# Two attention layers in one kernel: two pairs of scores in four banks under one exponential, the third pair first and copied

## The chip, the cores and the metric

The kernel runs on one core of one Trainium2 chip. The metric is device time in microseconds (us) of one launch, the median of the runs of a kernel. The engines are called as the profile's page calls them: PE (TensorE, matmuls), PEld (its weight loads), ACT (ScalarE), DVE (VectorE), POOL (GpSimd), SP (SyncE, which issues most DMAs).

## The reference

Two attention layers over 2048 tokens of 576 columns, 32 heads of 18, all in float32. Layer A has one key and value head shared by all query heads and no mask. Layer B has keys and values for every head, runs over four segments of 512 tokens with a causal mask inside a segment, and mixes in a memory of earlier segments. The two results stand side by side.

```python
# layer A
scores = jnp.einsum("bhqd,bkd->bhqk", q, k) * (Dh ** -0.5)
p = _softmax(scores, axis=-1)
o = jnp.einsum("bhqk,bkd->bhqd", p, v)
return (lambda x, *d: x.transpose(*d))(o, 0, 2, 1, 3).reshape(B, S, H * Dh) @ wo
...
# layer B, for each segment s
logits = jnp.einsum("bhqd,bhkd->bhqk", qs, ks) * scale + mask
p = _softmax(logits, axis=-1)
a_dot = jnp.einsum("bhqk,bhkd->bhqd", p, vs)
...
o = g * a_mem + (1.0 - g) * a_dot
...
return jnp.concatenate([a, b], axis=-1)
```

## The kernel before

The kernel has three stages. The first (up to about 281 us) projects queries, keys and values of both layers and builds B's memory. The second, attention, is the one that the change is in. The third (from about 1356 us) multiplies the last chunks by the output weights.

**Blocks and pairs.** Attention goes block by block. A block is four heads by 512 queries (`("A", c, hg)` or `("B", s, hg)`); there are 32 of each layer, and B's are put between A's early ones by the list `after`. A block of A has 16 key tiles of 128 keys. The four heads are two *pairs*, and the scores of one pair for one key tile are 128 x 1024 numbers (two heads by 512 queries) in two PSUM banks. So a block of A has 32 pairs. A block of B has three key tiles and six pairs. The mask leaves the first tile's pairs with 2 x 512 columns and the others' with 2 x 384, the third holding two short tiles side by side.

**Turns.** The pairs of a block are cut into *turns* of three. Since 32 is no multiple of three, a block of A has ten turns of three and a last one of two; a block of B has two turns. That makes 320 + 32 + 64 = 416 turns. `manual_schedule` fixes the order on PE, ACT and DVE as the loop over `k` writes it. In turn `k`:

- `scores` writes, for each pair, the score matmuls into a tile E of two banks (L890 for A, L898 for B). The pool `psE` has three such tiles, six of the eight banks. The other two are O (products) and F (other matmuls, one bank).
- The turn's second pair (`copied`) is copied by DVE from E to the SBUF tile W (L905), so that E is free before ACT gets to it. ACT then makes the exponential from W (L908). The first and third pairs are read by ACT straight from E (L908). ACT's order in a turn is first, third, second.
- In some places of A (`BY_DVE`: two fixed ones in each block, and a third where nothing else is due) DVE makes the exponential of half a pair itself, with seven operations on 512 columns (L864 to L871). ACT then takes only the other 512 columns, from W to the tile PD.
- B's exponentials are masked on the diagonal by POOL (L913).
- One step of other work follows from `run_fill` (mostly F: the output projection of finished chunks, L741, 8 matmul records a turn).
- Then the products of probabilities and values for the items of turn `k - 2` (`products`, L938): three items of four matmuls, each matmul in two records, into O. At a block's end DVE copies O out (L947).
- `due` places other steps that have become due: loads, sums, and POOL's weighing of finished heads (L725). A weighing step is held back near turns of B and while DVE's operations of an exponential are outstanding (`slow`).

Because the score of a turn goes into three tiles that come free one by one, PE may write the first pair of the next turn while ACT is still at this one's later pairs. Probabilities go to nine tiles P and two tiles PD, and the order of key tiles in the products (`turn_of`) lets DVE's slow ones come later.

Of the kernel before, what the change touches and what calls it, by code (L numbers as in the profile page):

```python
# [8 lines left out]
F32 = mybir.dt.float32  # L9
F32R = mybir.dt.float32r  # L10
# [22 lines left out]
BOUND_OK = 30.0 / SCALE / BOUND_UP  # L33
PBUFS = 9
KP = 54
# [13 lines left out]

LOG2 = SCALE * 1.4426950408889634  # L50
EXP_A = LOG2 * 2.0 ** 23
EXP_B = (127.0 + math.log2(0.00011720523372930181)) * 2.0 ** 23
POLY = [1.0925606709321247, 32.334180715292455, 88.7610992882796, 4291.093056129828]
MANTISSA, ONE_BITS, EXPONENT = 0x7FFFFF, 0x3F800000, 0xFF800000

BY_DVE = {(0, 1): 5, (5, 0): 12, (9, 1): 15}
THIRD = (9, 1)
QALL = [(slice(0, 36, 2), 0), (slice(1, 36, 2), 1), (slice(36, 54), 0)]
# [19 lines left out]
def attention_pair_kernel(ctx, tc, a_xT, a_w, a_wo, b_xT, b_w, b_wo, b_beta, ident_d, hmask_d, bmask_d, cmask_d, sel_d, zmask_d, selx_d, sely_d, out):  # L78
# [552 lines left out]
    pa = at_.enter_context(tc.tile_pool(name="pa", bufs=1, reuse_waits="tile"))  # L631
    psE = at_.enter_context(tc.tile_pool(name="psE", bufs=3, space=PSUM, reuse_waits="tile"))
    psO = at_.enter_context(tc.tile_pool(name="psO", bufs=1, space=PSUM, reuse_waits="tile"))
    attention = at_

# [220 lines left out]

    slow, now, gate, third = [], [0], [], set()
    AFTER = mybir.DependencyInfo(mybir.DependencyClass.Sync, mybir.DependencyReason.SCHED_ONLY)

    def exponentials(p, e, whole):  # L860

        u, w = (pp.tile([128, 512], F32, name=nm, bufs=1) for nm in "nq")
        v, stt, y = nc.vector, nc.vector.scalar_tensor_tensor, p.bitcast(U32)
        v.tensor_scalar(y, e, EXP_A, EXP_B, op0=ALU.mult, op1=ALU.add)  # L864
        ops = [
            lambda: v.tensor_scalar(u.bitcast(U32), y, MANTISSA, ONE_BITS, op0=ALU.bitwise_and, op1=ALU.bitwise_or),
            lambda: v.tensor_scalar(w.bitcast(U32), y, EXPONENT, None, op0=ALU.bitwise_and),
            lambda: stt(p, u, POLY[0], u, op0=ALU.add, op1=ALU.mult),
            lambda: stt(p, p, POLY[1], u, op0=ALU.add, op1=ALU.mult),
            lambda: stt(p, p, POLY[2], p, op0=ALU.add, op1=ALU.mult),  # L870
            lambda: stt(p, p, POLY[3], w, op0=ALU.add, op1=ALU.mult),  # L871
        ]
        slow.extend((now[0] + 2 + i, p, ops[2 * i : 2 * i + 2], whole) for i in range(3))

    def scores(it, pr, copied):

        ab, c, hg, kt = it
        st = stacks[ab, c, hg // 2]
        h = 2 * (hg % 2) + pr
        e = psE.tile([128, 2, 512], F32, name="E")  # L880
        if ab == "A" and (kt, pr) == THIRD and not any(cost and k <= now[0] + 4 for k, cost, *_ in later):
            third.add((c, hg))
        dve = ab == "A" and (kt, pr) in by_dve(c, hg)
        p = pp.tile([128, 2, 512], F32, name="PD" if dve else "P", bufs=2 if dve else PBUFS)
        state[it, pr] = p
        n = 512 if ab == "A" else 512 - 128 * kt if kt < 2 else 384
        if ab == "A":
            for j, r0 in enumerate(HALF):
                rows = slice(r0, r0 + KR)
                nc.tensor.matmul(e[:, j], kstA[rows, 128 * kt : 128 * kt + 128], st[rows, h, :], start=True, stop=True)  # L890
            if dve:
                exponentials(p[:, 0], e[:, 0], p)
        else:
            for k, c0 in BKEYS[kt]:
                ks = slice(128 * k, 128 * k + 128)
                for j, r0 in enumerate(HALF):
                    rows = slice(r0, r0 + KR)
                    nc.tensor.matmul(  # L898
                        e[:, j, c0 : c0 + 512 - 128 * k], st[rows, 4 + h, ks], st[rows, h, 128 * k :], start=True, stop=True
                    )  # L900
        src, hs = e, slice(0, 2)
        if copied:
            src = pp.tile([128, 2, 512], F32, name="W", bufs=2)
            hs = slice(1, 2) if dve else slice(0, 2)
            gate.append(nc.vector.tensor_copy(src[:, hs, :n], e[:, hs, :n]))  # L905

        def exponential():
            nc.scalar.activation(p[:, hs, :n], src[:, hs, :n], AF.Exp, scale=SCALE)  # L908
            if ab == "B":

                m = len(BKEYS[kt])
                diag = p.rearrange("p a (b t) -> p a b t", t=256)[:, :, 0:m, 0:128]
                nc.gpsimd.affine_select(  # L913
                    diag, diag, pattern=[[0, 2], [0, m], [1, 128]], base=0, channel_multiplier=-1, compare_op=ALU.is_ge, fill=0.0
                )

        return exponential

    acc, ready = {}, []

    def products(b, m, hf):
# [7 lines left out]
        for j in range(4):  # L929
            kt = turn_of(c, hg)[j // 2][m] if ab == "A" else m  # L930
            p = state[b + (kt,), j // 2]
            assert all(x[3] is not p for x in slow)
# [5 lines left out]
            nc.tensor.matmul(  # L938
                o[32 * j : 32 * j + 32, q0 : q0 + n],
                v,  # L940
                p[:, j % 2, p0 : p0 + n],
                start=m == hf == 0,
                stop=last and hf == 1,
            )
# [10 lines left out]
        return None  # L955


    def by_dve(c, hg):

        return [x for n, x in enumerate(BY_DVE) if n < 2 or (c, hg) in third]  # L960

    def turn_of(c, hg):

        order = []
        for pr in range(2):
            ks = [kt for kt in range(NKT) if (kt, pr) not in by_dve(c, hg)]
            for kt, p_ in by_dve(c, hg):
                if p_ == pr:
                    ks.insert(BY_DVE[kt, p_], kt)
            order.append(ks)  # L970
        return order

# [24 lines left out]
    def due(k, most=2, heavy=2):  # L997

        cost = 0

        near = [its[n][0] for t in turns[k : k + 3] for n, pr in t]
        heavy *= "B" not in near and not slow
        for e in [e for e in later if e[0] <= k]:
            if most and cost + e[1] <= heavy and e[2]():
                later.remove(e)
                e[3](k)
                cost += e[1]
                most -= 1
        return cost
# [66 lines left out]
    with tc.manual_schedule(engines={ENG.PE, ENG.Activation, ENG.DVE}):  # L1076
# [36 lines left out]
        def repeat(key):  # L1113

            o = parts[key]
            raws[key] = pp.tile([128, 2, 512], F32, name="PD", bufs=2)[:88, 0]
# [26 lines left out]
        def halve_heads(key, t):  # L1143
            R = RT[t]
            x = halves_of[key, t] = pp.tile([128, 2, 512], F32R, name="P", bufs=PBUFS)
            if t < 4:
                halve(x[:R, 0], x[:R, 1], parts[key][:R, t])
                return
            hi = pp.tile([128, 2, 512], F32R, name="PD", bufs=2)
            mixed(x[:, 0], hi[:, 0], parts[key][:, 4], some[:, 0:1])  # L1150
            mixed(x[:88, 1], hi[:88, 1], raws[key], some[:88, 1:2])

        for k in range(len(turns) + 2):
            now[0] = k
            exps = [scores(its[n], pr, i == 1) for i, (n, pr) in enumerate(turns[k])] if k < len(turns) else []
            for i in (0, 2, 1) if len(exps) == 3 else range(len(exps)):
                exps[i]()
            if k in (2, 4, 6):
# [17 lines left out]

            ends = k > 1 and any(hf and its[n][3] == (NKT - 1 if its[n][0] == "A" else 2) for n, hf in prods[k - 2])
            if slow and (slow[0][0] <= k or not ends):
# [73 lines left out]
        def eight_banks():  # L1252
            banks = [psE.tile([128, 2, 512], F32, name="E") for _ in range(3)]
            dst = [bk[:, hf, :288] for bk in banks for hf in range(2)]
            return dst + [psO.tile([128, C], F32, name=nm)[:, :288] for nm in ("O", "F")]

        def evict(osb, hf, src):
            (nc.vector.tensor_copy if hf else nc.scalar.copy)(osb[:, hf], src)

        dst = eight_banks()  # L1260
        for t in range(5):
# [17 lines left out]
        for g in range(8):  # L1279
# [4 lines left out]
            if not hf:  # L1284
                osb = pp.tile([128, 2, 512], F32, name="P", bufs=PBUFS)[:, :, :288]
            evict(osb, hf, dst[g])
# [234 lines left out]
```

## Time and profile before

| | |
|---|---|
| median of 3 runs | 1398.92 us (1397.57 to 1401.16) |
| the profiled execution | 1397.32 us, of which the span is 1395.4 us |
| granted TensorE clock | 0.999 |
| turns in attention | 416 |
| exponential instructions at L908 | 1216 (800 from E, 416 from W) |
| DVE's copies to W at L905 | 416 |

In the rows, `P<-E` is an instruction that writes P and reads E, with the shapes behind it, `x` the count, and the releaser of an idle time stands behind an arrow. Durations of neighbours on an engine can overlap, so the distance between two starts tells what one takes in a stream.

### The profile page before, as it was taken

How to read it: one execution, taken by the hardware profiler on the slowest of the kernel's cores; microseconds unless marked ns; L12 is line 12 of the kernel's file. 1: busy time of each engine (PE TensorE's matmuls, PEld its weight loads, DVE VectorE, ACT ScalarE, POOL GpSimd, SP SyncE). 2: the span in 40 equal slices, each digit the busy share in tenths (PEclk: the TensorE clock that was granted, in tenths of full speed). 3: DMA queues.
4: the chain of work that ended last, by engine and by line, in shares of the span. 5: the costliest groups of instructions: out<-in, count | busy, mean ns of one | idle time of the engine just before them, and what ended most of it. 6: DMA issues, size and time to landing. Idle time of an engine off the chain costs nothing.

```text
span 1395.4 us, 41198 instructions
## 1 busy us (share of the span) xinstructions
PE 1382.5 (99%) x17455; PEld 835.6 (60%) x17455; DVE 1033.2 (74%) x1512; ACT 1204.4 (86%) x1494; POOL 261.1 (19%) x382
## 2 busy tenths in 40 slices
PE   9999999999999999999999999999999999999998
PEld 6787887755554555555555555555555555555558
DVE  6655454477787788787888877876879778887884
ACT  4543553499999999999999999999999999999992
POOL 2443221003312211412110122113010220001002
PEclk9999999999999999999999999999999999999999
DMA  9766656576465445332312452232103321120013
GB/s 288 259 216 196 191 178 206 175 210 189 146 182 172 139 149 158 101 113 78 112 59 71 141 160 56 91 115 83 52 34 94 111 76 39 32 73 21 18 63 133
DMA packets 89022, 173.67 MB, mean 124 GB/s; under 512 B 12308, under 2 KB 20621, under 8 KB 88402
## 3 DMA queue, kind: packets, MB, share of 16 engines
q1 hardware_dynamic: 81902, 159.22, 36.6%
q0 software_dynamic: 2176, 6.51, 1.6%
q10 hardware_dynamic: 4752, 5.23, 1.1%
q8 instruction: 139, 2.28, 0.7%
q14 instruction: 53, 0.43, 0.1%
HBM read 99.65 MB, written 70.67 MB: 122 GB/s over the span
## 4 chain that ended last, share of the span: by engine, by line
PE 88%; DVE 5%; ACT 4%; issue 2%; DMA 1%; SPq 0%; POOL 0%; DVEq 0%; ACTq 0%
PE O L938 32%; PE E L890 20%; PE F L741 11%; PE pj L259 11%; ACT P L908 4%; PE E L898 3%; PE nd L496 2%; PE pj L496 2%; DVE W L905 2%; PE E L1222 2%; PE pj L291 1%; PE F L797 1%; PE tr L422 0%; DVE sm L690 0%; DMA stB<-qB 0%
## 5 line engine op out<-in xcount | busy, mean ns | idle before, releaser
L908 ACT ACTIVATE P<-E 128x1024 f32<-128x1024 f32 (+1 forms) x800 | 788.1, 1076 | 1.6 <-PE E L890 1.3
L905 DVE COPY W<-E 128x1024 f32<-128x1024 f32 (+2 forms) x416 | 453.2, 1089 | 143.1 <-PE E L890 84.2
L938 PE MATMUL O<-P,VA 128*32 128x256 f32 x7504 | 507.1, 379 | 0.0
L908 ACT ACTIVATE P<-W 128x1024 f32<-128x1024 f32 (+1 forms) x330 | 369.9, 1121 | 6.3 <-DVE W L905 5.6
L938 PEld LDWEIGHTS O<-P,VA 128*32 128x32 f32 x7504 | 259.0, 110 | 137.7 <-issue 4.3
L890 PE MATMUL E<-xl,kstA 56*128 56x512 f32 x1920 | 317.2, 430 | 2.1 <-ACT P L908 1.9
L890 PEld LDWEIGHTS E<-xl,kstA 56*128 56x128 f32 x1920 | 155.0, 184 | 159.1 <-issue 94.8
L913 POOL TENSOR_SCALAR_AFFINE_SELECT P<-P 128x256 f32<-128x256 f32 (+1 forms) x192 | 95.0, 495 | 412.5 <-ACT P L908 403.3
L725 POOL TENSOR_TENSOR xh<-xh,rb 126x512 f32<-126x512 f32 (+1 forms) x55 | 72.9, 1350 | 425.9 <-DVE PD L871 185.1
L741 PE MATMUL F<-woB,xh 126*32 126x192 f32 (+1 forms) x1920 | 126.6, 338 | 0.0
L938 PE MATMUL O<-PD,VA 128*32 128x256 f32 x688 | 88.9, 379 | 0.0
L741 PEld LDWEIGHTS F<-woB,xh 126*32 126x32 f32 (+1 forms) x1920 | 38.6, 108 | 74.9 <-issue 69.9
L938 PE MATMUL O<-P,vseg 128*32 128x256 f32 (+2 forms) x1536 | 81.4, 344 | 0.1
L947 DVE COPY oe<-O 128x512 f32<-128x512 f32 x64 | 44.3, 692 | 42.3 <-PE O L938 40.4
L259 PE MATMUL pj<-xh,wBl 128*126 128x512 f32 x180 | 71.9, 400 | 0.4 <-issue 0.4
L864 DVE TENSOR_SCALAR PD<-E 128x512 uint32<-128x512 f32 x86 | 59.2, 688 | 17.6 <-PE E L890 15.8
L259 PE MATMUL pj<-xh,wBh 128*126 128x512 f32 x180 | 71.6, 398 | 0.5 <-DVE xh L219 0.5
L124 ACT CAST qp<-pj 126x512 fp32r<-126x512 f32 (+1 forms) x54 | 31.1, 585 | 46.9 <-DVE kmB L454 41.8
L741 PE MATMUL F<-woA,xh 126*32 126x192 f32 (+1 forms) x960 | 63.9, 338 | 0.0
L938 PEld LDWEIGHTS O<-P,vseg 128*32 128x32 f32 x1536 | 48.8, 109 | 24.4 <-issue 1.9
L898 PE MATMUL E<-stB 56*128 56x256 f32 (+3 forms) x512 | 61.5, 348 | 2.0 <-ACT P L908 1.5
L871 DVE SCALAR_TENSOR_TENSOR PD<-PD,q 128x512 f32<-128x512 f32 x86 | 59.5, 692 | 3.0
(228 smaller groups left out, 1544.0 us busy)
## 6 DMA issues: line engine op xcount, KB each, us to landing
stB<-kB SPq DMA_DIRECT2D x96, 144.0 KB
stB<-qB SPq DMA_DIRECT2D x32, 288.0 KB
xl<-qA SPq DMA_DIRECT2D x30, 288.0 KB
oA<-oe SPq DMA_DIRECT2D x32, 256.0 KB
oB<-oe SPq DMA_DIRECT2D x32, 256.0 KB
qA<-qp SPq DMA_DIRECT2D x16, 504.0 KB
kB<-qp SPq DMA_DIRECT2D x16, 504.0 KB
qB<-qp SPq DMA_DIRECT2D x16, 504.0 KB
```

The source lines that it names most:

```text
L259: nc.tensor.matmul(dst, w[:, c0 : c0 + M], x, start=i == 0, stop=i == len(ops) - 1)
L496: nc.tensor.matmul(pj[:, :n], x, w, start=m == 0, stop=m == len(ops) - 1)
L725: ins = tc.keep_in_program_order(nc.gpsimd.tensor_tensor(dst, a, b, op=op))
L741: nc.tensor.matmul(dst[32 * j : 32 * j + 32], parts[ab, c][: RT[t], t, r0 : r0 + 32], wo[ab][: RT[t], t, c0 : c0 + n], start=start, stop=stop,
L864: v.tensor_scalar(y, e, EXP_A, EXP_B, op0=ALU.mult, op1=ALU.add)
L871: lambda: stt(p, p, POLY[3], w, op0=ALU.add, op1=ALU.mult),
L890: nc.tensor.matmul(e[:, j], kstA[rows, 128 * kt : 128 * kt + 128], st[rows, h, :], start=True, stop=True)
L898: nc.tensor.matmul(e[:, j, c0 : c0 + 512 - 128 * k], st[rows, 4 + h, ks], st[rows, h, 128 * k :], start=True, stop=True)
L905: gate.append(nc.vector.tensor_copy(src[:, hs, :n], e[:, hs, :n]))
L908: nc.scalar.activation(p[:, hs, :n], src[:, hs, :n], AF.Exp, scale=SCALE)
L913: nc.gpsimd.affine_select(diag, diag, pattern=[[0, 2], [0, m], [1, 128]], base=0, channel_multiplier=-1, compare_op=ALU.is_ge, fill=0.0)
L938: nc.tensor.matmul(o[32 * j : 32 * j + 32, q0 : q0 + n], v, p[:, j % 2, p0 : p0 + n], start=m == hf == 0, stop=last and hf == 1,)
```

## The change

The three tiles of two banks become one tile E2 of two banks and one tile E4 of four. In a turn of three pairs, two pairs of one key tile share E4, and the remaining pair has E2. `scores` takes the whole turn:

- The single pair is the third of the turn if the turn begins with a pair 0, else the first. Its matmuls come first. DVE copies it from E2 to W.
- Then the four score matmuls (for B's third tile eight) of the two others go into E4, and ACT makes one exponential over all four banks (2048 columns; 1536 for B's narrower tiles), from E4 to a tile P4.
- ACT's order in a turn is the wide exponential, then the one from W. A turn of two pairs has the wide one alone.
- POOL masks the wide pair in one instruction.
- DVE makes no exponentials: `exponentials`, `by_dve`, `turn_of`, the tables for them and the list `slow` are gone, and the products run in plain order of key tiles.

P becomes four tiles P4 and four tiles P2. Around the end, tiles that used the names P, PD and E take the new ones, and the output products get a pool of their own (`psN`) once the score banks are given back. The core of the diff:

```diff
-    def scores(it, pr, copied):
-
-        ab, c, hg, kt = it
-        st = stacks[ab, c, hg // 2]
-        h = 2 * (hg % 2) + pr
-        e = psE.tile([128, 2, 512], F32, name="E")
...
-        p = pp.tile([128, 2, 512], F32, name="PD" if dve else "P", bufs=2 if dve else PBUFS)
...
+    def scores(items):
+
+        pairs = [its[n] + (pr,) for n, pr in items]
+        single = [] if len(items) < 3 else [2 if items[0][1] == 0 else 0]
+        double = [i for i in range(len(items)) if i not in single]
+        todo = []
+        for group in (single, double):
+            if not group:
+                continue
+            w = 2 * len(group)
+            e = psE.tile([128, w, 512], F32, name=f"E{w}")
+            p = pp.tile([128, w, 512], F32, name=f"P{w}", bufs=PXBUFS if w == 4 else PBUFS)
...
+            for g, i in enumerate(group):
+                ab, c, hg, kt, pr = pairs[i]
...
+                state[its[items[i][0]], pr] = p[:, 2 * g : 2 * g + 2]
...
+                        e[:, 2 * g + j], kstA[rows, 128 * kt : 128 * kt + 128], st[rows, h, :], start=True, stop=True
...
+            src = e
+            if w == 2:
+                src = pp.tile([128, 2, 512], F32, name="W", bufs=2)
+                gate.append(nc.vector.tensor_copy(src[:, :, :n], e[:, :, :n]))
+            todo.append((p, src, n, w, len(BKEYS[kt]) if ab == "B" else 0))
+        for p, src, n, w, m in todo[::-1]:
+            nc.scalar.activation(p[:, :, :n], src[:, :, :n], AF.Exp, scale=SCALE)
...
-    psE = at_.enter_context(tc.tile_pool(name="psE", bufs=3, space=PSUM, reuse_waits="tile"))
+    psE = scored.enter_context(tc.tile_pool(name="psE", bufs=1, space=PSUM, reuse_waits="tile"))
...
-        heavy *= "B" not in near and not slow
+        heavy *= "B" not in near
...
-            for op in slow.pop(0)[2]:
-                gate.append(op())
```

How the instructions stand on PE in one turn of a block of A (c = 2, hg = 3, its fourth turn), with the engines that each first one waits for. Before, the turn's three pairs each have an E of their own, F follows, and then the products O:

```order
L890 MATMUL E_13342<-xl_11530,kstA_119 128x512 [waits Activation_49]
L890 MATMUL E_13342<-xl_11530,kstA_119 128x512
L890 MATMUL E_13346<-xl_11530,kstA_119 128x512 [waits DVE_49]
L890 MATMUL E_13346<-xl_11530,kstA_119 128x512
L890 MATMUL E_13355<-xl_11530,kstA_119 128x512 [waits Activation_49]
L890 MATMUL E_13355<-xl_11530,kstA_119 128x512
L741 MATMUL F_13250<-woB_4643,xh_10641 32x192 x4
```

Now (the next turn of the same block, in which the last product group stands behind a wait; E4 and E2 are the score tiles, P4 and P2 the probabilities):

```order
L875 MATMUL E2_12013<-xl_10400,kstA_119 128x512 [waits DVE_49]
L875 MATMUL E2_12013<-xl_10400,kstA_119 128x512
L875 MATMUL E4_12019<-xl_10400,kstA_119 128x512 [waits Activation_49]
L875 MATMUL E4_12019<-xl_10400,kstA_119 128x512 x3
L734 MATMUL F_11996<-woB_4421,xh_9630 32x192 x4
L916 MATMUL O_11968<-P4_11955,VA_120 32x256 x8
L916 MATMUL O_11968<-P2_11949,VA_120 32x256 x2
L916 MATMUL O_11968<-P2_11982,VA_120 32x256 [waits Activation_49]
L916 MATMUL O_11968<-P2_11982,VA_120 32x256
```

The copied pair moved from second to first, and the other two stand behind one wait for ACT. The last products read P2_11982, which ACT writes in the turn just before, as its last exponential.

On ACT, the same places. Before, two turns:

```order
L908 ACTIVATE P_13343<-E_13342 128x1024 [waits PE_49]
L908 ACTIVATE P_13356<-E_13355 128x1024 [waits PE_49,Activation_49]
L908 ACTIVATE PD_13347<-W_13353 128x512 [waits DVE_49]
L908 ACTIVATE P_13381<-E_13380 128x1024 [waits PE_49,Activation_49]
L908 ACTIVATE P_13391<-E_13390 128x1024 [waits PE_49]
L908 ACTIVATE P_13385<-W_13388 128x1024 [waits DVE_49]
```

Now, three turns:

```order
L891 ACTIVATE P4_11988<-E4_11987 128x2048 [waits PE_49,Pool_49]
L891 ACTIVATE P2_11982<-W_11985 128x1024 [waits DVE_49,Pool_49]
L891 ACTIVATE P4_12020<-E4_12019 128x2048 [waits PE_49,Activation_49]
L891 ACTIVATE P2_12014<-W_12017 128x1024 [waits DVE_49]
L891 ACTIVATE P4_12050<-E4_12049 128x2048 [waits PE_49,Activation_49]
L891 ACTIVATE P2_12044<-W_12047 128x1024 [waits DVE_49]
```

Three exponentials of a turn became two, and none of 512 columns is left.

More of the change, by code (lines that the diff above doesn't have):

```diff
@@ L854, in load_vseg @@
         vseg[s] = v
-    slow, now, gate, third = [], [0], [], set()
+    now, gate = [0], []
     AFTER = mybir.DependencyInfo(mybir.DependencyClass.Sync, mybir.DependencyReason.SCHED_ONLY)
[L860 to L873, printed above, removed]
@@ L875, in scores @@
-    def scores(it, pr, copied):
-        ab, c, hg, kt = it
-        st = stacks[ab, c, hg // 2]
-        h = 2 * (hg % 2) + pr
-        e = psE.tile([128, 2, 512], F32, name="E")
-        if ab == "A" and (kt, pr) == THIRD and not any(cost and k <= now[0] + 4 for k, cost, *_ in later):
-            third.add((c, hg))
-        dve = ab == "A" and (kt, pr) in by_dve(c, hg)
-        p = pp.tile([128, 2, 512], F32, name="PD" if dve else "P", bufs=2 if dve else PBUFS)
[L885 to L896, printed above, removed]
+    def scores(items):
[9 more added lines that the diff above has]
+            p = pp.tile([128, w, 512], F32, name=f"P{w}", bufs=PXBUFS if w == 4 else PBUFS)
+            ab, kt = pairs[group[0]][0], pairs[group[0]][3]
+            assert all((x[0], x[3]) == (ab, kt) for x in (pairs[i] for i in group))
+            n = 512 if ab == "A" else 512 - 128 * kt if kt < 2 else 384
+            for g, i in enumerate(group):
+                ab, c, hg, kt, pr = pairs[i]
+                st = stacks[ab, c, hg // 2]
+                h = 2 * (hg % 2) + pr
+                state[its[items[i][0]], pr] = p[:, 2 * g : 2 * g + 2]
+                for j, r0 in enumerate(HALF if ab == "A" else ()):
@@ L907, in exponential @@
[L907 to L911, printed above, removed]
+                for k, c0 in BKEYS[kt] if ab == "B" else ():
+                    ks = slice(128 * k, 128 * k + 128)
+                    for j, r0 in enumerate(HALF):
+                        rows = slice(r0, r0 + KR)
+                        nc.tensor.matmul(
+                            e[:, 2 * g + j, c0 : c0 + 512 - 128 * k], st[rows, 4 + h, ks], st[rows, h, 128 * k :], start=True, stop=True
+                        )
@@ L929, in products @@
         for j in range(4):
-            kt = turn_of(c, hg)[j // 2][m] if ab == "A" else m
+            kt = m
             p = state[b + (kt,), j // 2]
-            assert all(x[3] is not p for x in slow)
             k, p0, q0, n = (kt, 256 * hf, 256 * hf, 256) if ab == "A" else BHALF[kt][hf]
@@ L955, in products @@
         return None
[L958 to L971, printed above, removed]
     keys = {ab: list(dict.fromkeys((ab, c, hg // 2) for a_, c, hg in blocks if a_ == ab)) for ab in "AB"}
@@ L1154, in attention_pair_kernel @@
             now[0] = k
-            exps = [scores(its[n], pr, i == 1) for i, (n, pr) in enumerate(turns[k])] if k < len(turns) else []
-            for i in (0, 2, 1) if len(exps) == 3 else range(len(exps)):
-                exps[i]()
+            if k < len(turns):
+                scores(turns[k])
             if k in (2, 4, 6):
@@ L1252, in eight_banks @@
         def eight_banks():
-            banks = [psE.tile([128, 2, 512], F32, name="E") for _ in range(3)]
+            banks = [psN.tile([128, 2, 512], F32, name="E") for _ in range(3)]
             dst = [bk[:, hf, :288] for bk in banks for hf in range(2)]
@@ L1258, in evict @@
             (nc.vector.tensor_copy if hf else nc.scalar.copy)(osb[:, hf], src)
+        scored.close()
+        psN = at_.enter_context(tc.tile_pool(name="psN", bufs=3, space=PSUM, reuse_waits="tile"))
         dst = eight_banks()
```

35 lines of the change are left out of this document (13 added, 22 removed).

## The prediction

> **What bounds the kernel now.** I read the page first: busy time by engine, the 40 slices, the shares of the chain that ended last.
>
> ```profile
> PE 1382.5 (99%) x17455; PEld 835.6 (60%) x17455; DVE 1033.2 (74%) x1512; ACT 1204.4 (86%) x1494; POOL 261.1 (19%) x382
> ...
> PE   9999999999999999999999999999999999999998
> ...
> ACT  4543553499999999999999999999999999999992
> ...
> PEclk9999999999999999999999999999999999999999
> ...
> PE 88%; DVE 5%; ACT 4%; issue 2%; DMA 1%; SPq 0%; POOL 0%; DVEq 0%; ACTq 0%
> ```
>
> From slice 9 on, TensorE (PE) and ScalarE (ACT) are both full. The windows say the same in microseconds (columns: length, then each engine's busy time with its count, granted clock, DMA share):
>
> ```profile
> core 0: us, PE busy (x) PEld busy (x) DVE busy (x) ACT busy (x) POOL busy (x), PEclk, DMA share, GB/s
> 300.00:450.00 150.00, 146.30 (x1965) 76.51 (x1964) 116.71 (x155) 147.27 (x173) 36.97 (x68) 1.00 0.58 175
> 450.00:1050.00 600.00, 599.30 (x8796) 329.12 (x8788) 475.65 (x664) 597.43 (x685) 115.27 (x172) 1.00 0.33 100
> ```
>
> The change touches only the attention stage. The view of one line, L908, gives its ends (first and last start):
>
> ```profile
> L908 ACT ACTIVATE P<-E x800: 792/1080/1353, 281.3 to 1353.8; 128x1024 f32<-128x1024 f32 x146, 128x768 f32<-128x768 f32 x14
> ...
> L908 ACT ACTIVATE P<-W x330: 847/1126/1376, 286.1 to 1354.8; 128x1024 f32<-128x1024 f32 x153, 128x768 f32<-128x768 f32 x12
> ```
>
> The last exponential gives way to the next instruction 0.95 us after its start at 1354.8 (0.95 is shown below), so the stage lasts 1355.7 − 281.3 = 1074.4 us, in 416 turns: 2.58 us each. Three turns in the timeline:
>
> ```profile
> 901.32 0.97 PE L890 MATMUL E<-xl,kstA 56*128 56x512 f32 x6
> ...
> 902.22 0.53 PE L741 MATMUL F<-woA,xh 126*32 126x192 f32 x8
> 902.31 1.94 ACT L908 ACTIVATE P<-E 128x1024 f32<-128x1024 f32 x2
> ...
> 902.57 1.48 PE L938 MATMUL O<-P,VA 128*32 128x256 f32 x24
> ...
> 903.98 0.96 PE L890 MATMUL E<-xl,kstA 56*128 56x512 f32 x6
> 904.11 1.08 ACT L908 ACTIVATE P<-W 128x1024 f32<-128x1024 f32 x1
> ...
> 905.06 1.96 ACT L908 ACTIVATE P<-E 128x1024 f32<-128x1024 f32 x2
> ...
> 906.63 0.98 PE L890 MATMUL E<-xl,kstA 56*128 56x512 f32 x6
> ...
> 906.87 0.67 ACT L908 ACTIVATE PD<-W 128x512 f32<-128x512 f32 x1
> 907.39 1.98 ACT L908 ACTIVATE P<-E 128x1024 f32<-128x1024 f32 x2
> ```
>
> Starts matter here, not durations, since neighbours overlap. **ScalarE**: two exponentials from E take 904.11 − 902.31 = 1.80, so 0.90 each; one from W 905.06 − 904.11 = 0.95; a W of 512 columns 907.39 − 906.87 = 0.52. A turn is 2.75, and 2.33 where VectorE made half a pair. **TensorE**: from E to E 2.66 (901.32, 903.98, 906.63), made of E 0.90, F 0.35, and O 1.41 (three groups of 0.47). Both engines are within 4% of their limit, and three score buffers let one run ahead of the other by a turn. The waits between them are almost nothing (total us, times, longest):
>
> ```profile
> PE E L890 <- ACT P L908: 2.2, 12, 0.2
> ```
>
> ```profile
> ACT P L908 <- DVE W L905: 5.6, 12, 0.8
> ```
>
> **The change, part by part.**
>
> *VectorE's exponentials go.* They are this many half pairs (columns: count, busy us, mean ns):
>
> ```profile
> L908 ACT ACTIVATE PD<-W 128x512 f32<-128x512 f32 x86 | 61.3, 713 | 0.5 <-DVE W L905 0.5
> ```
>
> ScalarE gets 86 × (0.95 − 0.52) = 37 us more. VectorE is off the path already, so its relief is worth at most the stalls it caused ScalarE (5.6 us, above), and I take 4 of them as gained.
>
> *Two pairs in one exponential.* By the two W rows a column costs (0.95 − 0.52)/512 = 0.84 ns, so 2048 columns take 0.90 + 0.86 = 1.76 in a stream against 1.80 for two. That is 0.04 saved in each of the 384 turns with 2048 columns, 15 us. The trace has no such instruction. Its bounds are 1.72 (columns alone) and 1.80 (nothing saved); 1.76 is the line through the nearest rows. ScalarE's turn becomes 1.76 + 0.95 = 2.71, in every turn. The Trainium skill (ScalarE: Activation LUTs, What ACT_TABLE_LOAD costs) states 186 ns plus 0.833 per column, with neighbours overlapping by about 93 ns. That agrees with the W row (0.946 for 0.95) and not with the E row (0.946 for 0.90), so the row decides; by the page a merged exponential is an estimated 1.80, the turn 2.75, and the sum below 320 × 0.04 = 13 us higher.
>
> *One buffer of four banks.* This is the added wait. E4's first matmul must wait for the end of the turn before's exponential of 2048 columns, and the next exponential for all four matmuls. What that chain costs stands in two places of the timeline:
>
> ```profile
> 439.82 1.98 ACT L908 ACTIVATE P<-E 128x1024 f32<-128x1024 f32 x2
> ...
> 440.93 0.73 PE L890 MATMUL E<-xl,kstA 56*128 56x512 f32 x4
> ...
> 441.85 0.50 PE L890 MATMUL E<-xl,kstA 56*128 56x512 f32 x2 [0.18 <-ACT P L908]
> ```
>
> ```profile
> 283.65 0.96 PE L890 MATMUL E<-st,kstA 56*128 56x512 f32 x6
> ...
> 284.19 1.03 ACT L908 ACTIVATE P<-E 128x1024 f32<-128x1024 f32 x1 [0.44 <-PE E L890]
> ```
>
> The exponentials end at 439.82 + 1.98 = 441.80 and the waiting matmul starts at 441.85: 0.05. Four score matmuls take 0.73 from start to end, two take 0.50. At 283.65 the first two start, the exponential that waits for them starts 0.54 later: 0.04 after their 0.50. That exponential, with nothing before it, lasts 1.03; 2048 columns last 1.03 + 0.86 = 1.89. From one E4 exponential to the next the chain is 1.89 + 0.05 + 0.73 + 0.04 = **2.71**. ScalarE's own turn is 2.71, with W's exponential inside it, and TensorE's 2.66. Three limits lie within 0.05 of each other, and no buffer is left to average them: each turn pays the largest, plus what jitters. I take **2.74** for a turn of three pairs (0.03 over the largest, my choice). A block of A also has one turn of two pairs. It has no W, so nothing of ScalarE covers the way back, and it pays the chain's 2.71 though ScalarE works only 1.76.
>
> What is queued behind E4's wait on TensorE are F and all products of the turn, and behind those the next E2. F is in nearly all turns (8 matmuls a turn, 2880/8 = 360 of 416), so TensorE's 2.66 is the rule:
>
> ```profile
> L741 PE MATMUL F<-woB,xh 126*32 126x192 f32 (+1 forms) x1920 | 126.6, 338 | 0.0
> ...
> L741 PE MATMUL F<-woA,xh 126*32 126x192 f32 (+1 forms) x960 | 63.9, 338 | 0.0
> ```
>
> *The third pair first, through W.* VectorE's copy starts with E2, well before E4 is ready:
>
> ```profile
> L905 DVE COPY W<-E 128x1024 f32<-128x1024 f32 x298 | 364.0, 1222 | 110.0 <-PE E L890 84.2 <-ACT P L908 9.5 <-PE E L898 8.6
> ```
>
> Its 1.22 us lie under E4's matmuls (0.73) and exponential (1.89), so I cost it at nothing. Were that cover gone, W would come at most 1.22 late. Its exponential, though, now runs last of its turn, and every second turn the last product group needs the W of the turn just before. W ends 0.95 after E4's exponential; TensorE reaches that group 0.05 + 0.66 (two pairs up to F: 0.90 less a following pair's 0.73 − 0.50 = 0.23) + 0.35 + 0.94 = 2.00 after it, or 1.65 without F. Hidden by 0.7 at least in A.
>
> *Turns of B* (two per block, 32 blocks) are shorter and uneven:
>
> ```profile
> 657.13 0.90 PE L898 MATMUL E<-stB 56*128 56x512 f32 x6
> ...
> 659.29 1.10 PE L898 MATMUL E<-stB 56*128 56x384 f32 x10
> ...
> 659.73 0.53 PEld L898 LDWEIGHTS E<-stB 56*128 56x128 f32 x8 [0.25 <-ACT P L908]
> ...
> 662.09 0.91 PE L898 MATMUL E<-stB 56*128 56x512 f32 x6
> ```
>
> TensorE's two turns are 2.16 and 2.80, together 4.96. The second turn's E4 is the last eight of its ten matmuls, 1.10 − (659.73 − 659.29) = 0.66, so the chain is 1.89 + 0.05 + 0.66 + 0.04 = 2.64 into it, and out of it, with 512 columns fewer, 1.46 + 0.05 + 0.73 + 0.04 = 2.28: 4.92. If each turn pays the larger, 2.64 + 2.80 = 5.44. I take 5.1, nearer the sums. GpSimd's mask of the wide pair lies in this too:
>
> ```profile
> L913 POOL TENSOR_SCALAR_AFFINE_SELECT P<-P 128x256 f32<-128x256 f32 x128 | 54.1, 423 | 400.7 <-ACT P L908 395.2 <-POOL P L913 4.3 <-PE E L898 1.2
> ...
> L913 POOL TENSOR_SCALAR_AFFINE_SELECT P<-P 128x512 f32<-128x512 f32 x64 | 40.9, 640 | 11.8 <-ACT P L908 8.1 <-PE E L898 0.5 <-PE O L938 0.3
> ```
>
> At 217 ns per 256 columns the mask of 1024 lasts 1.07, and W's mask (0.42) stands behind it: done about 1.6 after E4's exponential, where TensorE wants it after 1.65 without F. Bounds 0 to 0.3 per block; inside my 5.1.
>
> *The sum.* Turns: 320 of three pairs of A, 32 of two, 64 of B. 320 × 2.74 + 32 × 2.71 + 32 × 5.1 = 876.8 + 86.7 + 163.2 = 1126.7, against 1074.4: +52.3, less 4 for stalls, **+48**. The tail after the stage does the same work from regrouped tiles: I take nothing (within 2 either way). The profiled execution took 1397.32 us, 1.6 under the median of the three runs; so 1446 for such an execution and **1447 us** as a median.
>
> **The rivals.**
>
> *TensorE becomes the bound.* While it waits for E4's bank it cannot load E4's weights ahead. A first pair takes 0.50, a following one 0.23; a turn that breaks in two pays between 0 and that 0.27 again. With half, and 0.05 for the semaphore, the turn is 2.66 + 0.13 + 0.05 = 2.84. For: TensorE is full. Against: the wait falls where ScalarE is busy. 320 × 2.84 + 86.7 + 32 × 5.3 = 1165, +91 − 4: **1486**.
>
> *ScalarE alone is the bound, and the kernel gets faster.* The place is E4's wait: if the way from one E4 exponential's end to the next's start (0.82 by the rows) hides under W's exponential and two-pair and B turns run ahead, turns cost 2.71, 1.76 and for B two E4 (1.76, 1.33) and two W of 768 columns (0.74 each), 4.57: 867.2 + 56.3 + 146.2 = 1069.7, −5, less the stalls −9: **1390**. It decides below a mean three-pair turn of (1074.4 − 86.7 − 163.2)/320 = 2.58 with the other turns as forecast, which W's own 0.95 and 2048 columns at their floor of 1.72 (2.67) forbid. So it needs the chain gone also where no W covers it. Against it speaks every row above.
>
> *TensorE's clock falls* because it idles a little in every turn. In the window 300 to 450 it idled 3.7 of 150 us and the granted clock stayed 1.00; forecast idling is 0.08 of 2.74. At half the clock a turn costs 2.66 more; in a tenth of the turns that is 42 × 2.66 = 112: **1559**. The Trainium skill (TensorE: Matmul & The Clock Gate, A second HAM failure mode: psum-queue depth-cycling) speaks against this change here: it tells of short idling between matmul groups, as PSUM banks cycle, that made the clock swing between full and half; no row here shows it.
>
> That the change does not do what it says is excluded by the instruction rows: the wide exponentials stand there.
>
> **How the numbers follow.** Chances: forecast 0.74, TensorE the bound 0.17, ScalarE alone or a part of it 0.07, clock 0.02. Ends of the forecast: low, a turn at ScalarE's and the chain's bare 2.71 with 1.72 for the exponential (2.67), B at 4.92: 320 × 2.67 + 86.7 + 157.4 = 1098.5, +24 − 4: 1419; high, 2.81 and 5.44: 1160, +86: 1483. Both ends together are unlikely, so the range is **1425 to 1482**; below it lies 0.07, above it about 0.11. A difference of 0.3% (4 us) is about what a measurement of this kernel tells from no change. Faster by more: 0.04; within: 0.03; slower by more: 0.93.
>
> **What would show it.** Right: ACT's starts 2.70 to 2.76 apart from wide to wide, also across the turn of two pairs; idle time on ScalarE before wide exponentials put down to E's matmuls; TensorE's idle time at E put down to P, hundreds of times; VectorE's busy time well down with nothing gained. Wrong: wide exponentials 2.58 or less apart; or TensorE without gaps and 2.8 apart; a clock under 1.00. The forecast falls if a wide exponential costs clearly more or less than 1.76, or if the way back is not 0.82.

## The result and the profile after

| | before | after |
|---|---|---|
| median | 1398.68 us (1397.57 to 1401.16, 4 runs) | 1460.70 us (1460.43 to 1463.49, 4 runs) |
| ratio | | 1.0445, 95% interval 1.0426 to 1.0464 |
| the profiled execution | 1397.32 us | 1460.95 us (span 1459.2) |

The kernel became 62 us slower. The forecast was 1447, range 1425 to 1482.

The page of the changed kernel, with the lines that answer to those shown of before:

```profile
PE 1422.4 (97%) x17455; PEld 832.9 (57%) x17455; DVE 707.8 (49%) x878; ACT 1236.1 (85%) x1078; POOL 246.2 (17%) x318
...
PE   9999999999999999999999999999999999999998
...
ACT  4543543699999999999999999999999999999992
...
PEclk9999999999999999999999999999999999999999
...
ACT 57%; PE 35%; issue 5%; DMA 1%; DVE 1%; POOL 0%; ACTq 0%; DVEq 0%
```

The slices look the same: TensorE and ScalarE full, the clock too. VectorE's 325 us less have bought nothing. Only the chain that ended last has changed sides: PE had 88% of it, now ACT has 57%. The timeline shows why (start, length, engine; two turns of three pairs and the start of the next):

```profile
941.66 1.88 ACT L891 ACTIVATE P<-E 128x2048 f32<-128x2048 f32 x1
...
943.25 1.07 PE L875 MATMUL E<-xl,kstA 56*128 56x512 f32 x6
943.43 1.05 ACT L891 ACTIVATE P<-W 128x1024 f32<-128x1024 f32 x1
943.59 0.30 PEld L875 LDWEIGHTS E<-xl,kstA 56*128 56x128 f32 x4 [0.16 <-ACT P L891]
...
944.25 0.53 PE L734 MATMUL F<-woB,xh 126*32 126x192 f32 x8
944.42 1.88 ACT L891 ACTIVATE P<-E 128x2048 f32<-128x2048 f32 x1
...
944.60 1.48 PE L916 MATMUL O<-P,VA 128*32 128x256 f32 x24
...
946.01 1.07 PE L875 MATMUL E<-xl,kstA 56*128 56x512 f32 x6
946.20 1.05 ACT L891 ACTIVATE P<-W 128x1024 f32<-128x1024 f32 x1
946.35 0.30 PEld L875 LDWEIGHTS E<-xl,kstA 56*128 56x128 f32 x4 [0.16 <-ACT P L891]
...
947.19 1.88 ACT L891 ACTIVATE P<-E 128x2048 f32<-128x2048 f32 x1
```

A turn is 944.42 − 941.66 = 2.76. Follow the chain: the wide exponential ends at 941.66 + 1.88 = 943.54; E4's weights load at 943.59, 0.05 later; the score matmuls end at 943.25 + 1.07 = 944.32, 0.73 later; the next wide exponential starts at 944.42, **0.10** later. Sum 1.88 + 0.05 + 0.73 + 0.10 = 2.76. Note what the page does not show: between W's exponential and the wide one ScalarE has no idle time in its row, because W's (943.43 to 944.48) is still counted as running when the wide one starts. That it waited is seen in the starts alone: 944.42 − 943.43 = 0.99, where before the change an exponential from W gave way after 0.95.

Where no W lies in between, in the turn of two pairs, the same wait is plain idle time:

```profile
1001.78 1.88 ACT L891 ACTIVATE P<-E 128x2048 f32<-128x2048 f32 x1
1004.55 1.88 ACT L891 ACTIVATE P<-E 128x2048 f32<-128x2048 f32 x1 [0.89 <-PE E L882]
```

Here too 2.77 pass, though ScalarE has only 1.88 to do. On TensorE's side, the matmuls stood idle for ScalarE as follows (total us, times, longest; L875 writes A's scores, L882 B's). Before, A's row was 2.2 us in 12 times:

```profile
PE E L875 <- ACT P L891: 17.9, 70, 0.6
PE E L882 <- ACT P L891: 8.5, 21, 0.7
```

The view of line L875 alone gives a larger number, because it counts weight loads that wait as well:

```profile
  ACT P L891: 106.0, 394
```

That number says little about the chain: the run further down with three separate score tiles has 113.4 us in 365 times there.

From the trace's starts I summed the time from each turn's first exponential to the next turn's, by kind of turn (31 turns of two pairs, since the last turn of all ends the stage):

| us | 320 of three pairs | 31 of two | 64 of B |
|---|---|---|---|
| before | 856.1 (2.68 each) | 65.8 (2.12) | 150.7 (2.35) |
| after | 885.0 (2.77) | 86.4 (2.79) | 164.1 (2.56) |
| difference | +28.9 | +20.6 | +13.4 |

Together +62.9. The tail after attention is unchanged within 0.2, and the first exponential starts 1.1 later. Of that, 0.4 is the wait for six matmuls instead of two (1.33 us from the first score matmul's start, 0.93 before); the other 0.7 is a later end of the first stage, which varies from run to run by as much without the change (the kernel before without VectorE's exponentials has its first exponential 1.9 later).

### The profile page after: what moved, and what is told of

Read it like the earlier page. It is cut to its first block, busy times and chain, and to the rows that moved or that the text cites. A ratio compares the mean times of both kernels' runs of the same rounds, so it can differ in the third digit from the quotient of the medians.

```text
span 1459.2 us, 39871 instructions
## 1 busy us (share of the span) xinstructions
PE 1422.4 (97%) x17455; PEld 832.9 (57%) x17455; DVE 707.8 (49%) x878; ACT 1236.1 (85%) x1078; POOL 246.2 (17%) x318
## 4 chain that ended last, share of the span: by engine, by line
ACT 57%; PE 35%; issue 5%; DMA 1%; DVE 1%; POOL 0%; ACTq 0%; DVEq 0%
ACT P L891 57%; PE pj L251 10%; PE O L916 6%; PE E L875 4%; PE E L882 4%; PE nd L488 2%; PE F L734 2%; PE pj L488 2%; PE E L1184 2%; PE pj L283 1%; PE tr L414 0%; DMA gt<-b_beta 0%; DMA wBl<-a_w 0%; PE mm L428 0%; PE F L1184 0%
## 5 line engine op out<-in xcount | busy, mean ns | idle before, releaser
L891 ACT ACTIVATE P<-E 128x2048 f32<-128x2048 f32 (+1 forms) x416 | 767.5, 1845 | 40.2 <-PE E L875 18.4
L888 DVE COPY W<-E 128x1024 f32<-128x1024 f32 (+1 forms) x384 | 452.5, 1178 | 501.8 <-PE E L875 400.8
L891 ACT ACTIVATE P<-W 128x1024 f32<-128x1024 f32 (+1 forms) x384 | 389.7, 1015 | 0.0
L875 PE MATMUL E<-xl,kstA 56*128 56x512 f32 x1920 | 349.0, 457 | 16.4 <-ACT P L891 16.2
L916 PEld LDWEIGHTS O<-P,VA 128*32 128x32 f32 x8192 | 263.0, 109 | 147.2 <-issue 5.8
L875 PEld LDWEIGHTS E<-xl,kstA 56*128 56x128 f32 x1920 | 154.2, 184 | 200.0 <-issue 102.3
L894 POOL TENSOR_SCALAR_AFFINE_SELECT P<-P 128x256 f32<-128x256 f32 (+2 forms) x128 | 82.5, 655 | 479.8 <-ACT P L891 476.1
L882 PE MATMUL E<-stB 56*128 56x256 f32 (+3 forms) x512 | 68.3, 359 | 9.1 <-ACT P L891 8.5
L882 PEld LDWEIGHTS E<-stB 56*128 56x128 f32 x512 | 38.2, 185 | 43.6 <-ACT P L891 20.2
L251 PE MATMUL pj<-xl,wBh 128*126 128x512 f32 x144 | 57.5, 399 | 0.0
L117 DVE TENSOR_TENSOR qp<-pj,qp 126x512 fp32r<-126x512 f32 (+1 forms) x54 | 36.8, 688 | 31.8 <-ACT qp L116 31.2
```

What stands on the lines that cost most here:

```text
L117: hold(nc.vector.tensor_tensor(qp[:R, 1, :n], src, qp[:R, 0, :n].bitcast(F32), op=ALU.subtract))
L251: nc.tensor.matmul(dst, w[:, c0 : c0 + M], x, start=i == 0, stop=i == len(ops) - 1)
L875: nc.tensor.matmul(e[:, 2 * g + j], kstA[rows, 128 * kt : 128 * kt + 128], st[rows, h, :], start=True, stop=True)
L882: nc.tensor.matmul(e[:, 2 * g + j, c0 : c0 + 512 - 128 * k], st[rows, 4 + h, ks], st[rows, h, 128 * k :], start=True, stop=True)
L888: gate.append(nc.vector.tensor_copy(src[:, :, :n], e[:, :, :n]))
L891: nc.scalar.activation(p[:, :, :n], src[:, :, :n], AF.Exp, scale=SCALE)
```

## The experiments

Three theories stood against each other. **C**: the chain through the single four-bank buffer sets each turn. **S**: ScalarE is the bound, and the lost help is the whole loss. **T**: TensorE is the bound, since it must break in the middle of its scores. Medians below are of four runs each, ratios against the kernel before on the same chip.

### VectorE's exponentials alone

The kernel before, without them:

```diff
-BY_DVE = {(0, 1): 5, (5, 0): 12, (9, 1): 15}
+BY_DVE = {}
```

> The kernel before with no exponentials on VectorE, everything else as before (three score tiles of two banks). Theory C (the changed kernel is set by the chain from wide exponential to E4's matmuls to wide exponential, through the one buffer): the lost help alone makes every three-pair turn ScalarE's 2.76 us and leaves B's and the two-pair turns (68 and 151 us together) as they are: 320 x 2.76 + 68 + 151 = 1102 against 1074, so 1425, plus or minus 8. Rival S (ScalarE is the bound, the loss of VectorE's help is the whole loss): about 1460. Rival T (TensorE is the bound once it waits in the middle of the scores): no statement on the size, but the loss would appear only with E4.

Measured: 1422.3 us, ratio 1.0170 (1.0147 to 1.0193). S falls as the whole account: the lost help is 25 us, not 62. Its turns of three pairs sum to 882.4, or 2.758 each. So most of the +28.9 in those turns is lost help (26.3), and not the chain, which stands only 0.01 above it.

### The four banks as two tiles

```diff
-            e = psE.tile([128, w, 512], F32, name=f"E{w}")
+            es = [psE.tile([128, 2, 512], F32, name=f"E{w}{x}") for x in "ab"[: len(group)]]
...
+                e = es[g]
...
-            nc.scalar.activation(p[:, :, :n], src[:, :, :n], AF.Exp, scale=SCALE)
+            for g, x in enumerate(src):
+                nc.scalar.activation(p[:, 2 * g : 2 * g + 2, :n], x[:, :, :n], AF.Exp, scale=SCALE)
```

> The changed kernel with the four banks as two tiles of two banks, each released by its own exponential; order, copy and lack of VectorE's exponentials as in the change. Theory C: the chain is gone and the time is that of the lost help alone, the same as the kernel before without VectorE's exponentials, 1425 plus or minus 10. Rival S: 1455 to 1470. Rival T (order of the scores with the copied pair first costs TensorE): 1455 or more.

Measured: 1434.65 us, ratio 1.0267 (1.0245 to 1.0290), at the upper edge of what C expected. With each exponential releasing its own two banks, 26 of the 62 us come back, though ScalarE makes one more instruction in each turn. It is 12 us over the run before it, and nearly all of that lies in the turns of two pairs: 73.9 us against 62.2, with 882.2 and 882.4 in those of three.

### The same three tiles in rotation

The remaining 12 us could be the order, or the fixed place of each tile. Against the run before it:

```diff
-    psE = scored.enter_context(tc.tile_pool(name="psE", bufs=1, space=PSUM, reuse_waits="tile"))
+    psE = scored.enter_context(tc.tile_pool(name="psE", bufs=3, space=PSUM, reuse_waits="tile"))
...
-            es = [psE.tile([128, 2, 512], F32, name=f"E{w}{x}") for x in "ab"[: len(group)]]
+            es = [psE.tile([128, 2, 512], F32, name="E") for _ in group]
```

> The kernel with three score tiles, copied pair first, without VectorE's exponentials, but the three tiles taken in rotation as in the kernel before instead of one fixed tile for each place in the turn. Theory (a turn of two pairs leaves the fixed tile E2 unused, so TensorE cannot run ahead and pays its own 2.4 us in each): two-pair turns fall from 2.39 to about 2.0 us, 12 less, 1422 (1418 to 1427), the time of the kernel before without VectorE's exponentials. Rival (what costs is that no pair of a two-pair turn is copied, or the order): unchanged, 1432 to 1437.

Measured: 1427.14 us, ratio 1.0204 (1.0186 to 1.0221), a hair over the expected 1418 to 1427. Two-pair turns fell from 73.9 to 63.4 us, as the theory of the fixed places has it. B's turns gave some back (152.7 to 156.1), whose cause was not followed, so 7.5 of the 12 us came back in all. The other 5 stay open.

### Two exponentials on the same four banks

This undoes the merge alone and leaves the chain.

```diff
-            nc.scalar.activation(p[:, :, :n], src[:, :, :n], AF.Exp, scale=SCALE)
+            for g in range(0, w, 2):
+                nc.scalar.activation(p[:, g : g + 2, :n], src[:, g : g + 2, :n], AF.Exp, scale=SCALE)
```

> The changed kernel with the wide exponential made as two of 1024 columns on the same four banks. Theory C: the chain gets longer by what two take more than one from the first start to the last end, 1.94 against 1.88, in all turns: 384 x 0.06 = +23, so 1483 (1475 to 1490). Rival S: ScalarE's turn grows by 0.04 but stands 0.05 under the measured turn: 1460 to 1474. Rival T: unchanged, 1461.

Measured: 1487.42 us, ratio 1.0639 (1.0616 to 1.0662), 27 us over the change. Its turns of three pairs are 2.829: the 0.06 by which two exponentials last longer from first start to last end appears whole. The merge does gain what it can, but only within the chain that the shared banks made.

### ScalarE's work cut

W's exponential on 64 of each head's columns; the rest of the single pair keeps its scores, so most exponentials of a third of the pairs are left out.

```diff
-                src = pp.tile([128, 2, 512], F32, name="W", bufs=2)
+                src = p
...
-            nc.scalar.activation(p[:, :, :n], src[:, :, :n], AF.Exp, scale=SCALE)
+            x = 64 if w == 2 else n
+            nc.scalar.activation(p[:, :, :x], src[:, :, :x], AF.Exp, scale=SCALE)
```

> The changed kernel with W's exponential cut to 64 of each head's columns, made in place in the probability tile (the other columns of the single pair keep their scores, so that part of the softmax is left out). ScalarE works 0.80 us less in each three-pair turn. Theory C: nothing of it is gained, 1456 to 1466, wide exponentials still 2.76 apart. Rival S: the turn falls to TensorE's 2.66 or the chain, at least 25 us less, 1436 or lower. Rival T: unchanged as with C.

Measured: 1459.69 us, ratio 1.0444 (1.0422 to 1.0465): the change's own time. Its page and timeline:

```profile
PE 1422.6 (98%) x17455; PEld 833.4 (57%) x17455; DVE 705.5 (48%) x878; ACT 981.1 (67%) x1078; POOL 246.4 (17%) x318
```

```profile
943.60 1.88 ACT L892 ACTIVATE P<-E 128x2048 f32<-128x2048 f32 x1 [0.68 <-PE E L875]
...
945.37 0.30 ACT L892 ACTIVATE P<-P 128x128 f32<-128x128 f32 x1
...
946.36 1.88 ACT L892 ACTIVATE P<-E 128x2048 f32<-128x2048 f32 x1 [0.69 <-PE E L875]
```

ScalarE works 255 us less, stands idle 0.69 us in each turn, and the turn is still 946.36 − 943.60 = 2.76. An engine that the change's page shows full was not its bound. This is the clearest of the runs against S. T, which expected the same, is left to the runs below.

### One wait instead of two

In the trace of the change, an instruction that only waits stands ahead of 412 of the 416 wide exponentials, since these wait for two things: E4's matmuls, and the old contents of its probability tile (the row of ACT's order shows `[waits PE_49,Activation_49]`). The edit makes W's exponential, which has time, wait for an exponential late enough to cover the next wide one's second wait.

```diff
+            ins = nc.scalar.activation(p[:, :, :n], src[:, :, :n], AF.Exp, scale=SCALE)
+            if w == 4:
+                wide.append(ins)
+            elif len(wide) > 2:
+                tc.add_manual_dep(ins.ins, wide[-3].ins.name, AFTER, reason="W's exponential takes the wait for the buffer of the next wide one")
```

> The changed kernel in which W's exponential takes the wait for the buffer of the next wide one, so that the wide exponential has one wait (for TensorE) instead of two. In the trace of the change it starts 0.10 us after the last score matmul's end, with an instruction of its own for one of the waits between, where the forecast had 0.04. Theory C: the chain falls from 2.76 by 0.06 to 2.70, and ScalarE's own 2.715 takes over: 320 x 0.045 + 32 x 0.06 + some 2 for B = 18 less, 1443 (1438 to 1448). Rivals S and T: unchanged, 1458 to 1464.

Measured: 1443.49 us, ratio 1.0316 (1.0298 to 1.0335).

```profile
942.50 1.05 ACT L891 ACTIVATE P<-W 128x1024 f32<-128x1024 f32 x1
943.45 1.87 ACT L891 ACTIVATE P<-E 128x2048 f32<-128x2048 f32 x1
945.22 1.05 ACT L891 ACTIVATE P<-W 128x1024 f32<-128x1024 f32 x1
946.17 1.87 ACT L891 ACTIVATE P<-E 128x2048 f32<-128x2048 f32 x1
```

The turn is 946.17 − 943.45 = 2.72, and W gives way after 943.45 − 942.50 = 0.95 again. S and T, which said unchanged, fall. The 17 us are the 0.06 that the forecast's chain had missed, of which ScalarE's own turn leaves 0.04.

The waits themselves tell more than was expected. Most were not moved but are gone: in the change 348 wide exponentials carry a wait for ScalarE's own earlier work, here only 62 exponentials from W do. And 64 wide ones keep a second wait, for GpSimd. These still start 0.10 us after the last matmul's end, the other 352 only 0.05 after it (medians), and turns of three pairs in A that lead to the one kind last 2.77, to the other 2.71. So the price of the second wait shows inside one run too.

### The same matmuls in the chain and beside it

One more pair of 128 columns, which writes the last pair's first columns again, in A's turns; in the first run into E4, in the second into E2 (`w == 2`, there with the single pair's columns):

```diff
+            if w == 4 and ab == "A":
+                for j, r0 in enumerate(HALF):
+                    rows = slice(r0, r0 + KR)
+                    nc.tensor.matmul(
+                        e[:, w - 2 + j, :128], kstA[rows, 128 * kt : 128 * kt + 128], st[rows, h, :128], start=True, stop=True
+                    )
```

> The changed kernel with one more pair of score matmuls in A's turns, 128 columns wide, that writes the last pair's first 128 columns once more into E4, so within the chain. TensorE works some 0.1 us more in each turn of A. Theory C: all of it is paid, 352 x 0.06 to 0.15 = 21 to 53 more, about 1495. Rival S: ScalarE's 2.715 hides 0.05 of it: 0 to 30 more. Rival T: all of it is paid, here and beside the chain alike.

> The same additional pair of 128 columns, but into E2, ahead of E4's wait and so beside the chain. TensorE's own turn becomes about 2.76. Theory C: free, 1458 to 1468. Rival T: as much as in the chain, 1482 to 1514. Rival S: free.

Measured: 1481.89 us in the chain (ratio 1.0591, 1.0572 to 1.0609) and 1464.38 beside it (1.0472, 1.0450 to 1.0494): 21 us over the change, and 4. Turns of three pairs are 2.825 and 2.774 against 2.766. The 21 are the low edge of C's 21 to 53 and lie within S's 0 to 30 too, so it is the pair of runs that decides. The same work on the same engine costs 21 us in E4 and 4 in E2, so T falls: TensorE has room, though its row is 97% full. The 4 us are no more than what runs of one kernel differ by (the two intervals of the ratio overlap), and were not followed.

### The turn of two pairs split

Two exponentials of one pair each, the second through E2 and W:

```diff
-        single = [] if len(items) < 3 else [2 if items[0][1] == 0 else 0]
+        single = [1] if len(items) < 3 else [2 if items[0][1] == 0 else 0]
...
+            z = 2 if group is single else 4
...
-            nc.scalar.activation(p[:, :, :n], src[:, :, :n], AF.Exp, scale=SCALE)
+            nc.scalar.activation(p[:, :w, :n], src[:, :w, :n], AF.Exp, scale=SCALE)
```

> The changed kernel with the turns of two pairs split: the first pair in two banks of E4 with an exponential of 1024 columns, the second through E2 and W. Theory C: the chain out of that turn is 1.03 + 0.05 + 0.73 + 0.10 = 1.91 in place of 2.76, and W covers ScalarE's wait: 32 x 0.85 = 27 less, 1434 (1428 to 1442). Rival S: ScalarE works 0.09 more in each of these turns: 1461 to 1464. Rival T: unchanged, 1461.

Measured: 1449.12 us, ratio 1.0363 (1.0344 to 1.0382): 12 us gained, not 27. The turn fell from 2.79 to 2.44 and not to 1.91. The timeline of one:

```profile
1284.18 0.85 PE L876 MATMUL E<-xl,kstA 56*128 56x512 f32 x4
...
1284.96 0.53 PE L734 MATMUL F<-woB,xh 72*32 72x192 f32 x8
1285.31 1.48 PE L917 MATMUL O<-P,VA 128*32 128x256 f32 x24
1285.32 1.02 ACT L892 ACTIVATE P<-E 128x1024 f32<-128x1024 f32 x1
1286.22 1.06 ACT L892 ACTIVATE P<-W 128x1024 f32<-128x1024 f32 x1
1286.72 0.96 PE L876 MATMUL E<-xl,kstA 56*128 56x512 f32 x6
```

The turn has two pairs of scores, but F and three full groups of products like any other: TensorE takes 1286.72 − 1284.18 = 2.54 for it, and the next E4 stands behind that: ScalarE has left E4 at 1285.32 + 1.02 = 1286.34, but TensorE comes back to the scores only at 1286.72. Here TensorE is the next limit, and the expectation had left it out. In the kernel before, rotating tiles let it run ahead and such a turn cost 2.12.

### Both mends

> The changed kernel with both mends, the one wait of the wide exponential and the split turn of two pairs. Theory C, with TensorE's own 2.43 us as the floor of a split turn (seen in the run with the split alone, 2.44 in place of the expected 1.91): the gains of the two add, 17 and 12 us, 1432 (1427 to 1438). Still above the kernel before, since ScalarE has no help.

Measured: 1432.84 us, ratio 1.0243 (1.0226 to 1.0260). The gains add. None of the versions tried reaches the kernel before. By the sums of starts, turns of three pairs keep 15 us over it (2.72 against 2.68 on the mean, where VectorE helped), those of two 8, and B's 12. Cutting the chain further would still leave ScalarE's own 2.71 in every turn of three pairs.

## Why the prediction was right, and where it was off

**The mechanism was right.** A chain through the single E4 sets A's turns: a turn stays 2.76 with ScalarE's work cut by 255 us, grows by what is put into the chain and by little of what is put beside it, and shrinks when one of the chain's links is cut. Its links were forecast as 1.89, 0.05, 0.73 and 0.04, and measured as 1.88, 0.05, 0.73 and 0.10.

**The link that was mis-sized** is the last, from the end of E4's matmuls to the start of the exponential. The 0.04 came from the exponential at 284.19, which had one wait; nearly all wide ones have two, and that costs 0.06 more. (The first four wide ones of the changed kernel have one wait, and 0.04.) The order rows of the change, shown above, name both waits of each wide exponential; the prediction had them and did not price them. The 0.03 added for jitter covered half of it by luck: turns of three pairs were forecast at 2.74 and are 2.766 (+8 us in the sum). Actual jitter is small; nine tenths of these turns lie between 2.755 and 2.775.

**The other terms.** Turns of two pairs: forecast 2.71, measured 2.79 (+2). B: forecast 163.2, measured 164.1 (+1), or 5.13 a block between the 4.92 and 5.44 of the working. With 0.10 for the last link, the chain gives 1.88 + 0.05 + 0.66 + 0.10 = 2.69 into B's second turn and 1.45 + 0.05 + 0.73 + 0.10 = 2.33 out of it; the starts are 2.71 and 2.42 apart, so B's turns lie near the chain as well, though no run tested that alone. The 4 us of stalls ought not to have been taken off (+4): the new turns were priced whole, and the stalls of before stand only in the 1074.4 that was subtracted. The first exponential is 1.1 later, which was not in the sum (+1). 8 + 2 + 1 + 4 + 1 = 16 is what the profiled executions differ by beyond the forecast (63.6 − 48). A slip without consequence: by its own terms the high end is 1481, not 1483.

**The merge** was forecast to bring ScalarE's turn from 2.75 to 2.71. The wide exponential gives way to W after 943.43 − 941.66 = 1.77 in the change, against 1.76 forecast, and with the chain out of the way (one wait) the turn is 2.72. So the gain exists, some 0.035 a turn, and the chain's last 0.06 took it. By the Trainium skill (ScalarE: Activation LUTs, What ACT_TABLE_LOAD costs) a lone one takes an estimated 1.89 and one in a stream an estimated 1.80; the trace has 1.88 for its length and 1.77 to the next start.

**What the sum did not separate.** The prediction put the turn of three pairs down to the chain. It is the chain that binds, but without it the lost help alone would give 2.758. Divided by the runs, of the 62 us about 25 are the lost help, 12 came with the new order and the fixed places of the tiles, and 26 with the shared release of four banks (by the ratios 24, 14 and 25). Of the 12, taking the tiles in rotation brought 7.5 back; the rest has no run of its own. Of the 26, by the sums of starts against the run with three fixed tiles, 12.5 lie in turns of two pairs (86.4 − 73.9), 11.4 in B's (164.1 − 152.7) and 2.8 in turns of three (885.0 − 882.2).

**Of the signs named beforehand**, the starts from wide to wide came at 2.76, and at 2.77 across the turn of two pairs shown (2.79 on the mean), a little over the 2.70 to 2.76. VectorE's busy time fell with nothing gained, and the clock stayed full. The way back, of which the prediction says that the forecast falls if it is not 0.82, was 0.88: the missing 0.06 again. TensorE's waits for P came hundreds of times only in the view that counts weight loads, and without the chain they are as many, so this sign decides nothing. ScalarE's idle time before wide exponentials did not show in the turns of three pairs, where W's row covers it; only the turns of two pairs and B show it (36 us in 60 times, from the table of ScalarE's waits):

```profile
ACT P L891 <- PE E L875: 18.4, 30, 0.9
ACT P L891 <- PE E L882: 17.6, 30, 1.2
```

**The rivals.** TensorE as the bound would have shown the same price for the pair beside the chain; it showed 4 us where the pair in the chain showed 21. ScalarE alone is excluded by its cut work. The clock stayed 1.00 in the changed kernel, also early in attention, where TensorE idled most:

```profile
300.00:450.00 150.00, 142.34 (x1906) 73.19 (x1902) 78.66 (x88) 144.85 (x110) 32.34 (x46) 1.00 0.57 173
```

It idled 7.7 of 150 us there without a slower clock. What the Trainium skill (TensorE: Matmul & The Clock Gate, A second HAM failure mode: psum-queue depth-cycling) tells of a clock that swings where TensorE idles briefly between groups as PSUM banks cycle did not show here: the granted clock is 1.00 in this window and in the two behind it.

## What to carry to other kernels

Merging two instructions of a consumer saves one fixed price (0.04 us here) but also merges the release of their buffers; where the producer refills what the consumer releases, write down the loop consumer, signal, producer, signal, and compare it with each engine's own turn, also in the turns that have nothing to cover it. A row that is full does not prove a bound: cut a part of its work and see if the time moves. On such a loop, count the waits of each instruction, and let an earlier instruction that has time cover the ones that are long satisfied.

## What the runs showed of the hardware

- A ScalarE instruction with two waits started 0.10 us after the end of the matmul that it waited for, with one wait 0.04 to 0.05; with the second wait off most wide exponentials, 17 us of 1461 came back.
- One exponential of 2048 columns over four PSUM banks lasts 1.88 us from its start, where two of 1024 take 1.94 from first start to last end, and W's exponential starts 1.77 after its start.
- An activation that waits under the tail of its predecessor leaves no idle time in the profile: W's row of 1.05 reached past the next start, and only the distance of the starts (0.99 for 0.95) told of the wait.
